# Delta-rule recurrence and gated experts on one core: gates' exponential and rank comparison ordered four slots later, softmax sums of two experts inverted together

## The chip, the cores and the metric

The kernel runs on 1 core of a Trainium2 chip. The metric is the device time of one execution in microseconds, the median of several runs. Engines are named as the profile names them: PE is TensorE, DVE VectorE, ACT ScalarE, POOL GpSimd, SP the engine that issues transfers.

## The reference

A recurrence over 768 steps, for 4 batches of 8 heads, gives `x` of 4 x 768 x 320. Then four small attention experts work on `x`; each row (token) uses the two experts with the largest gate:

```python
logits = x @ w_gate
topk = np.argpartition(-logits, K, axis=-1)[..., :K]     # K = 2 of E = 4
sel = sel - sel.max(-1, keepdims=True)
w = np.exp(sel)
w /= w.sum(-1, keepdims=True) + 1e-09
for e in range(E):
    scores = scale * (q @ k.transpose(0, 2, 1))          # causal
    a = np.exp(scores - scores.max(-1, keepdims=True))
    a /= a.sum(-1, keepdims=True) + 1e-09
    out += mask[..., None] * w[:, :, kk:kk + 1] * (a @ v @ wo[e])
```

## The kernel before

The first part, `recurrence`, computes `x` in chunks up to about 385 us of the profiled execution; its order is written out by hand and the change leaves it alone. The second part, `moe`, is the experts.

**Units.** The experts' work is 48 units, one for each batch b (4), block j of 256 rows (3) and expert e (4), in the order of `UNITS`; units 2p and 2p+1 are always the two experts of one pair, an even and an odd one, with the same rows. A unit has two row tiles t. For each, `scores` (L806) multiplies queries and keys into a PSUM tile `sc` (two buffers), VectorE adds the causal mask and takes the row's extreme (L813, which frees `sc`), and ScalarE takes the exponential with the row's sum (L815). `norm` then adds 1e-9 to the two sums (L820), inverts them (L821), GpSimd multiplies the inverse by the token's gate (L822) and the whole tile `P` by the result (L826, two multiplications of 128 to 768 columns). TensorE transposes `P` (L834) three units later, ScalarE (L840) or VectorE (L838) copies the transposes to SBUF, and four units later `mix` (L852) multiplies them with the values, for both experts of the pair at once. `fin` (L863) applies the output weights.

**Batch preparation.** While the units of one batch run, the pieces of the next batch's projections are filled in between (`FILL`): `l`/`s` load and split `x` (VectorE cast L706, then GpSimd L707 and L708), `k` the queries and keys (L729, copied out of PSUM by ScalarE L737 and VectorE L738), `v` the values and the gates' logits (L748, L751, L752). All of them and the transposes share three PSUM buffers named `pt`.

**The gates.** For a batch, `rank` compares the four logits of each token with one another on VectorE (L766) and counts on GpSimd how many are larger (L768, L770, nine small additions and subtractions after one another, "the counts" below); `shift` takes the maximum (L774), subtracts it on GpSimd (L775) and turns the counts into a 0/1 choice on VectorE (L776, "the comparison"); `gate` takes the exponential on ScalarE (L779), multiplies by the choice on GpSimd (L780), and VectorE sums and inverts (L781 to L783) before GpSimd scales (L784). Batch 0 does this in two halves, the others once each.

**The order.** Each piece of the program is a slot; `later(d, f)` places an operation d slots after the one that asks for it, with `DL, DE, DN, DR` as the distances. From this written order the compiler's scheduler makes one fixed queue for each engine, in which an operation may stand earlier or later than written; at run time every engine works through its queue in order and waits where an operand isn't ready.

```python
LAG = (3, 4, 6)
DL, DE, DN, DR = 1, 3, 4, 1
            later(DE, lambda: A.activation(P[:, 0:n], P[:, 0:n], AF.Exp, bias=m[:, 0, t:t + 1], scale=-1.0, accum_out=m[:, 1, t:t + 1]))
            if t == 1:
                later(DN, norm)
```

Of the kernel before, what the change touches and what calls it, by code (L numbers as in the profile page):

```python
# [7 lines left out]
F32 = mybir.dt.float32  # L8
AF = mybir.ActivationFunctionType
OP = mybir.AluOpType  # L10
# [580 lines left out]

DL, DE, DN, DR = 1, 3, 4, 1

# [64 lines left out]
def moe(tc, ctx, I, xT, out, ident, pre, FL=None, FI=None):  # L658
# [10 lines left out]
    def later(d, f):  # L669
        due.setdefault(now[0] + d, []).append(f)  # L670
# [45 lines left out]
    def proj(b):  # L716
# [37 lines left out]
        gs = {}  # L754
        def rank(a, i=slice(0, 6)):

            L = G[b][:, i]
            if a == 0:
                gs["R"] = sp.tile([128, 6, 4], F32, name="gr", bufs=2)
                gs["c"] = sp.tile([128, 3, 6, 3], F32, name="gc", bufs=1)  # L760
                gs["m"] = sp.tile([128, 2, 6], F32, name="gm", bufs=2)
                for d in range(4):
                    PL.memset(gs["R"][:, i, d], 3.0 - d)
            R, c = gs["R"][:, i], gs["c"][:, a, i]
            n = c.shape[1]
            V.tensor_tensor(c[:, :, 0:3 - a], L[:, :, a:a + 1].to_broadcast([128, n, 3 - a]), L[:, :, a + 1:4], op=OP.is_ge)  # L766
            def count():
                PL.tensor_tensor(R[:, :, a + 1:4], R[:, :, a + 1:4], c[:, :, 0:3 - a], op=OP.add)  # L768
                for d in range(3 - a):
                    PL.tensor_tensor(R[:, :, a], R[:, :, a], c[:, :, d], op=OP.subtract)  # L770
            later(DR, count)
        def shift(i=slice(0, 6)):
            L, R, mx = G[b][:, i], gs["R"][:, i], gs["m"][:, 0, i]
            V.tensor_reduce(mx, L, axis=AX.X, op=OP.max)  # L774
            PL.tensor_tensor(L, L, mx[:, :, None].to_broadcast(L.shape), op=OP.subtract)  # L775
            V.tensor_scalar(R, R, 1.5, None, op0=OP.is_lt)  # L776
        def gate(i=slice(0, 6)):
            L, R, mx, c = G[b][:, i], gs["R"][:, i], gs["m"][:, 0, i], gs["m"][:, 1, i]
            A.activation(L, L, AF.Exp)  # L779
            PL.tensor_tensor(L, L, R, op=OP.mult)  # L780
            V.tensor_reduce(mx, L, axis=AX.X, op=OP.add)  # L781
            V.tensor_scalar(mx, mx, 1e-9, None, op0=OP.add)
            V.reciprocal(c, mx)  # L783
            PL.tensor_tensor(L, L, c[:, :, None].to_broadcast(L.shape), op=OP.mult)  # L784
        half = lambda x: slice(3 * x, 3 * x + 3)
# [3 lines left out]

    OT, PT = {}, {}  # L790

    def unit(b, j, e, last):
# [3 lines left out]
        def scores(t):  # L796
# [10 lines left out]
            if t == 0:  # L807
                st["m"] = sp.tile([128, 4, 2], F32, name="m", bufs=10)
                st["P"] = [None, None]
            m = st["m"]  # L810
            P = st["P"][t] = sp.tile([128, 768], F32, name="P", bufs=8)
# [3 lines left out]
            later(DE, lambda: A.activation(P[:, 0:n], P[:, 0:n], AF.Exp, bias=m[:, 0, t:t + 1], scale=-1.0, accum_out=m[:, 1, t:t + 1]))  # L815
            if t == 1:
                later(DN, norm)
        def norm():
            m = st["m"]
            V.tensor_scalar(m[:, 2], m[:, 1], 1e-9, None, op0=OP.add)  # L820
            V.reciprocal(m[:, 2], m[:, 2])  # L821
            PL.tensor_tensor(m[:, 3], m[:, 2], G[b][:, 2 * j:2 * j + 2, e], op=OP.mult)  # L822
            for t in range(2):
                n = 128 * (2 * j + t + 1)
                P = st["P"][t]
                PL.tensor_tensor(P[:, 0:n], P[:, 0:n], m[:, 3, t:t + 1].to_broadcast([128, n]), op=OP.mult)  # L826
        def transp(z):
# [149 lines left out]
```

## Time and profile before

| what | value |
|---|---|
| time, median of 3 runs | 623.82 us (622.46 to 625.45) |
| the profiled execution's own time | 622.29 us |
| its span, first to last instruction | 620.5 us |
| mean granted TensorE clock | 0.942 of full speed |
| busy over the span: TensorE, VectorE, ScalarE, GpSimd | 88%, 75%, 77%, 59% |

All rows below come from that one profiled execution, whose own time is 1.53 us below the median. Times in rows are microseconds from the span's start. A timeline row gives the start, the duration (of merged rows, from the first start to the last end), engine, line, operation, tiles, count, and in brackets the engine's idle time before it and what ended that.

### The profile page before, as it was taken

The numbers are of one execution on the slowest core, as the hardware profiler recorded it, in microseconds if no ns is written. First come the engines' busy times: TensorE is split into PE (matmuls) and PEld (weight loads), VectorE is DVE, ScalarE is ACT, GpSimd is POOL, SyncE is SP. The second block draws the span as 40 slices with busy tenths as digits, with TensorE's granted clock in tenths as the row PEclk, the third lists the DMA queues.
The fourth block names the chain that finished last, engine by engine and source line by source line (L and its number), as shares of the span: only waits on it lengthen the run. The fifth ranks groups of instructions, "written<-read, shape, count | busy, mean of one in ns | idle before, by whom it ended". The sixth has DMA issues, their size and how long they took to land.

```text
span 620.5 us, 22307 instructions
## 1 busy us (share of the span) xinstructions
PE 545.8 (88%) x8753; PEld 477.8 (77%) x8753; DVE 468.5 (75%) x1137; ACT 478.9 (77%) x1299; POOL 366.0 (59%) x600
## 2 busy tenths in 40 slices
PE   5564799998898889889999999889999979999996
PEld 5454688887787778778888778768888868888884
DVE  7977768899999979997567773776785567567752
ACT  7992569899879878988999995677775577677763
POOL 2321299759968989998880020586854646463851
PEclk9555579999999999999999999999999989999999
DMA  7884344676578566646338943432131132202111
GB/s 198 226 191 109 99 108 117 140 202 157 121 178 208 141 143 186 155 102 183 88 94 242 235 115 111 109 90 64 50 109 38 50 80 58 69 1 52 43 37 57
DMA packets 63690, 73.77 MB, mean 119 GB/s; under 512 B 30168, under 2 KB 48344, under 8 KB 63576
## 3 DMA queue, kind: packets, MB, share of 16 engines
q1 hardware_dynamic: 63432, 72.15, 45.1%
q8 instruction: 72, 1.18, 0.8%
q14 instruction: 42, 0.34, 0.2%
q10 hardware_dynamic: 144, 0.10, 0.1%
HBM read 54.92 MB, written 11.01 MB: 106 GB/s over the span
## 4 chain that ended last, share of the span: by engine, by line
PE 51%; ACT 19%; POOL 10%; DVE 10%; issue 6%; DMA 4%; SPq 0%; POOLq 0%; DVEq 0%; ACTq 0%
PE py L415 6%; PE ot L852 6%; PE pt L729 6%; PE sc L806 4%; PE pt L834 4%; PE pt L863 4%; PE pt L748 3%; POOL MT L319 3%; POOL TP L319 3%; PE pt L441 3%; ACT GT L386 3%; PE ps L392 3%; ACT LS L445 3%; PE ps L405 3%; PE ps L383 3%
## 5 line engine op out<-in xcount | busy, mean ns | idle before, releaser
L319 POOL TENSOR_TENSOR MT<-MT,TP 128x30 f32<-128x30 f32 (+9 forms) x150 | 99.2, 662 | 11.8
L319 POOL TENSOR_TENSOR TP<-MT 128x30 f32<-128x30 f32 (+9 forms) x150 | 92.1, 614 | 11.6
L826 POOL TENSOR_TENSOR P<-P,m 128x128 f32<-128x128 f32 (+2 forms) x96 | 88.5, 943 | 3.5
L415 PE MATMUL py<-R,LS 128*40 128x80 f32 x1536 | 85.4, 238 | 3.4 <-issue 0.8
L813 DVE CUSTOM_DVE_ANT_0 P<-sc,MK 128x128 f32<-128x128 f32 (+2 forms) x96 | 59.5, 623 | 24.3 <-PE sc L806 14.5
L408 DVE TENSOR_TENSOR R<-ps,CM 64x128 f32<-64x128 f32 x192 | 54.9, 286 | 23.7 <-PE ps L405 20.1
L415 PEld LDWEIGHTS py<-R,LS 128*40 128x40 f32 x1536 | 63.8, 119 | 11.6 <-ACT LS L445 5.3
L815 ACT ACTIVATE P<-P,m 128x128 f32<-128x128 f32 (+2 forms) x96 | 63.8, 665 | 11.5 <-DVE m L813 10.7
L806 PE MATMUL sc<-ks,qs 128*128 128x384 f32 (+4 forms) x256 | 61.2, 343 | 1.9 <-DVE m L813 1.9
L394 ACT ACTIVATE R<-ps 32x160 f32<-32x160 f32 x192 | 56.6, 295 | 5.6 <-PE ps L392 1.5
L386 ACT ACTIVATE GT<-ps 32x160 f32<-32x160 f32 x192 | 56.4, 294 | 3.4
L834 PE MATMUL pt<-CM,P 128*128 128x128 f32 x336 | 52.6, 277 | 6.3 <-ACT pt L840 5.1
L822 POOL TENSOR_TENSOR m<-m,gg 128x2 f32<-128x2 f32 x48 | 10.8, 224 | 78.1 <-DVE m L821 54.8
L392 PE MATMUL ps<-GT,TT 128*33 128x80 f32 x768 | 47.0, 244 | 3.3 <-DVE TT L321 1.3
L376 ACT ACTIVATE LS<-pt 64x320 f32<-64x320 f32 x96 | 41.4, 432 | 9.8 <-PE pt L372 8.3
L834 PEld LDWEIGHTS pt<-CM,P 128*128 128x128 f32 x336 | 40.1, 141 | 11.4 <-ACT pt L840 6.2
L405 PE MATMUL ps<-RB,VU 128*64 128x64 f32 x768 | 46.1, 229 | 3.0 <-ACT VU L400 1.9
L445 ACT ACTIVATE LS<-pt 40x320 f32<-40x320 f32 x92 | 39.6, 430 | 10.8 <-PE pt L441 7.8
L806 PEld LDWEIGHTS sc<-ks,qs 128*128 128x128 f32 x256 | 40.8, 191 | 4.1 <-DVE m L813 3.1
L729 PE MATMUL pt<-xh,wq 128*128 128x384 f32 x192 | 41.5, 349 | 2.0 <-DVE xh L706 1.2
L405 PEld LDWEIGHTS ps<-RB,VU 128*64 128x64 f32 x768 | 36.1, 139 | 8.6 <-ACT VU L400 7.8
L283 PE MATMUL ps<-AB,KB 40*64 40x32 f32 x512 | 26.3, 274 | 18.5 <-DVE AB L258 12.8
(159 smaller groups left out, 1346.6 us busy)
## 6 DMA issues: line engine op xcount, KB each, us to landing
RB<-in_RB SPq DMA_DIRECT2D x24, 320.0 KB
EK<-in_EK SPq DMA_DIRECT2D x18, 416.0 KB
ks<-ks SPq DMA_DIRECT2D x32, 192.0 KB
R<-in_VG SPq DMA_DIRECT2D x24, 208.0 KB
EW<-in_EA SPq DMA_DIRECT2D x18, 214.5 KB
R<-in_VT SPq DMA_DIRECT2D x48, 80.0 KB
R<-in_RT SPq DMA_DIRECT2D x24, 160.0 KB
xT<-XT SPq DMA_DIRECT2D x48, 80.0 KB
```

The costliest lines, as they stand in the source:

```text
L319: return [lambda: e.tensor_tensor(tmp, row, col, op=OP.mult), lambda: e.tensor_tensor(o, o, tmp, op=OP.add)]
L386: A.activation(gt[b:b + 32, s::2], p_g[64 * s:64 * s + 32], AF.Copy)
L392: T.matmul(p_u[64 * x:64 * x + 33, y], tt[:, o:o + 33], gt[:, 2 * p:2 * p + 2], start=True, stop=True, tile_position=(0, 64 * x))
L405: T.matmul(p_f[64 * x:64 * x + 64, y], vu[:, p, :], rb[:, 4 * g + p, :], start=True, stop=True, tile_position=(0, 64 * x))
L415: T.matmul(py[64 * s:64 * s + 40, p], ls[:, h, :], m, start=True, stop=True, tile_position=(0, 64 * s))
L445: A.activation(o, x, AF.Copy)
L729: T.matmul(p, w, x, start=(j == 0), stop=(j == len(prs) - 1))
L806: T.matmul(ps[:, c, 0:cw], QS[b][:, e, o], KS[b][:, e, z, k], start=(z == 0), stop=(z == 1))
L813: V.tensor_tensor_reduce(pv, ps[:, 0:ch, 0:cw], MK[:, 768 - n:768].rearrange("p (c k) -> p c k", c=ch), 1.0, 3e38, OP.add, OP.min, m[:, 0, ...
L815: later(DE, lambda: A.activation(P[:, 0:n], P[:, 0:n], AF.Exp, bias=m[:, 0, t:t + 1], scale=-1.0, accum_out=m[:, 1, t:t + 1]))
L826: PL.tensor_tensor(P[:, 0:n], P[:, 0:n], m[:, 3, t:t + 1].to_broadcast([128, n]), op=OP.mult)
L834: T.transpose(p[:, 128 * y:128 * y + 128], st["P"][t][:, 128 * c:128 * c + 128], ident)
```

## The change

In the gates, the counts are no longer placed one slot after each comparison of logits but are written by `shift` itself, after the subtraction of the maximum; the exponential (L779 before, L776 after) and the comparison (L776 before, L777 after) are placed `DR` = 4 slots later, the multiplication by the choice 4 slots after `gate`'s own slot, and sum, inverse and scaling 8 slots after it. In the units, `norm` is no longer called for each unit but once for a pair, by the odd one: 1e-9, inverse and product with the gates act on four sums of the pair, and GpSimd then multiplies the even unit's two tiles and after them the odd unit's.

```diff
@@ -589,7 +589,7 @@
 
 LAG = (3, 4, 6)
 
-DL, DE, DN, DR = 1, 3, 4, 1
+DL, DE, DN, DR = 1, 3, 4, 4
 
 FIRST = "l1 k1 v0 k0 s1 v2 v1 R0 R1 R2 k2 H0 k3 G0"
 FILL0 = "k4 k7", "k6 v4 k5", "v3", "v5 R3 R4 R5 H1", "G1", "", "", "", "", "", "", ""
@@ -764,30 +764,34 @@
             R, c = gs["R"][:, i], gs["c"][:, a, i]
             n = c.shape[1]
             V.tensor_tensor(c[:, :, 0:3 - a], L[:, :, a:a + 1].to_broadcast([128, n, 3 - a]), L[:, :, a + 1:4], op=OP.is_ge)
-            def count():
-                PL.tensor_tensor(R[:, :, a + 1:4], R[:, :, a + 1:4], c[:, :, 0:3 - a], op=OP.add)
-                for d in range(3 - a):
-                    PL.tensor_tensor(R[:, :, a], R[:, :, a], c[:, :, d], op=OP.subtract)
-            later(DR, count)
         def shift(i=slice(0, 6)):
             L, R, mx = G[b][:, i], gs["R"][:, i], gs["m"][:, 0, i]
             V.tensor_reduce(mx, L, axis=AX.X, op=OP.max)
             PL.tensor_tensor(L, L, mx[:, :, None].to_broadcast(L.shape), op=OP.subtract)
-            V.tensor_scalar(R, R, 1.5, None, op0=OP.is_lt)
+            for a in range(3):
+                c = gs["c"][:, a, i]
+                PL.tensor_tensor(R[:, :, a + 1:4], R[:, :, a + 1:4], c[:, :, 0:3 - a], op=OP.add)
+                for d in range(3 - a):
+                    PL.tensor_tensor(R[:, :, a], R[:, :, a], c[:, :, d], op=OP.subtract)
+            later(DR, lambda: A.activation(L, L, AF.Exp))
+            later(DR, lambda: V.tensor_scalar(R, R, 1.5, None, op0=OP.is_lt))
         def gate(i=slice(0, 6)):
             L, R, mx, c = G[b][:, i], gs["R"][:, i], gs["m"][:, 0, i], gs["m"][:, 1, i]
-            A.activation(L, L, AF.Exp)
-            PL.tensor_tensor(L, L, R, op=OP.mult)
-            V.tensor_reduce(mx, L, axis=AX.X, op=OP.add)
-            V.tensor_scalar(mx, mx, 1e-9, None, op0=OP.add)
-            V.reciprocal(c, mx)
-            PL.tensor_tensor(L, L, c[:, :, None].to_broadcast(L.shape), op=OP.mult)
+            def pick():
+                PL.tensor_tensor(L, L, R, op=OP.mult)
+            def total():
+                V.tensor_reduce(mx, L, axis=AX.X, op=OP.add)
+                V.tensor_scalar(mx, mx, 1e-9, None, op0=OP.add)
+                V.reciprocal(c, mx)
+                PL.tensor_tensor(L, L, c[:, :, None].to_broadcast(L.shape), op=OP.mult)
+            later(DR, pick)
+            later(2 * DR, total)
         half = lambda x: slice(3 * x, 3 * x + 3)
         return dict(l=lambda n: load(b, n), s=lambda n: split(b, n), k=lambda i: qk((0, 2, 1, 3)[i % 4], i // 4)(), v=lambda i: vg(i)(),
                     r=rank, h=lambda i: shift(), g=lambda i: gate(), R=lambda x: rank(x % 3, half(x // 3)),
                     H=lambda x: shift(half(x)), G=lambda x: gate(half(x)))
 
-    OT, PT = {}, {}
+    OT, PT, PAIR = {}, {}, {}
 
     def unit(b, j, e, last):
 
@@ -805,25 +809,28 @@
                 for z in range(2):
                     T.matmul(ps[:, c, 0:cw], QS[b][:, e, o], KS[b][:, e, z, k], start=(z == 0), stop=(z == 1))
             if t == 0:
-                st["m"] = sp.tile([128, 4, 2], F32, name="m", bufs=10)
+                if s == 0:
+                    PAIR[b, j, ep] = (sp.tile([128, 4, 2, 2], F32, name="m", bufs=4), [])
                 st["P"] = [None, None]
-            m = st["m"]
+                PAIR[b, j, ep][1].append(st["P"])
+            m = PAIR[b, j, ep][0][:, :, s]
             P = st["P"][t] = sp.tile([128, 768], F32, name="P", bufs=8)
             pv = P[:, 0:n].rearrange("p (c k) -> p c k", c=ch)
             V.tensor_tensor_reduce(pv, ps[:, 0:ch, 0:cw], MK[:, 768 - n:768].rearrange("p (c k) -> p c k", c=ch), 1.0, 3e38,
                                    OP.add, OP.min, m[:, 0, t:t + 1])
             later(DE, lambda: A.activation(P[:, 0:n], P[:, 0:n], AF.Exp, bias=m[:, 0, t:t + 1], scale=-1.0, accum_out=m[:, 1, t:t + 1]))
-            if t == 1:
+            if t == 1 and s == 1:
                 later(DN, norm)
         def norm():
-            m = st["m"]
+            m, Ps = PAIR[b, j, ep]
             V.tensor_scalar(m[:, 2], m[:, 1], 1e-9, None, op0=OP.add)
             V.reciprocal(m[:, 2], m[:, 2])
-            PL.tensor_tensor(m[:, 3], m[:, 2], G[b][:, 2 * j:2 * j + 2, e], op=OP.mult)
-            for t in range(2):
-                n = 128 * (2 * j + t + 1)
-                P = st["P"][t]
-                PL.tensor_tensor(P[:, 0:n], P[:, 0:n], m[:, 3, t:t + 1].to_broadcast([128, n]), op=OP.mult)
+            PL.tensor_tensor(m[:, 3], m[:, 2], G[b][:, 2 * j:2 * j + 2, 2 * ep:2 * ep + 2].rearrange("p t e -> p e t"), op=OP.mult)
+            for x in range(2):
+                for t in range(2):
+                    n = 128 * (2 * j + t + 1)
+                    P = Ps[x][t]
+                    PL.tensor_tensor(P[:, 0:n], P[:, 0:n], m[:, 3, x, t:t + 1].to_broadcast([128, n]), op=OP.mult)
         def transp(z):
 
             if z == 0:
```

What this does to the engines' queues is shown at three places (lines of the changed kernel: L766, L769, L777, L783 to L785 are the gates on VectorE, L770, L773, L775 on GpSimd; L819 is the mask, L828 and L833 the products with the gate and with `P`).

GpSimd where the gates of the third batch are made (about 485 to 497 us of the trace), before:

```order
L826 TENSOR_TENSOR P<-P,m 128x640
L826 TENSOR_TENSOR P<-P,m 128x768
L822 TENSOR_TENSOR m<-m,gg 128x2
L826 TENSOR_TENSOR P<-P,m 128x640
L826 TENSOR_TENSOR P<-P,m 128x768
L707 TENSOR_TENSOR xh<-x,xh 64x384
L708 TENSOR_TENSOR x<-x,xh 128x768
L768 TENSOR_TENSOR gr<-gr,gc 128x6x3
```

and after the change:

```order
L707 TENSOR_TENSOR xh<-x,xh 64x384
L828 TENSOR_TENSOR m<-m,gg 128x4
L708 TENSOR_TENSOR x<-x,xh 128x768
L833 TENSOR_TENSOR P<-P,m 128x640
L833 TENSOR_TENSOR P<-P,m 128x768
L833 TENSOR_TENSOR P<-P,m 128x640
L833 TENSOR_TENSOR P<-P,m 128x768
L770 TENSOR_TENSOR gg<-gg,gm 128x24
L773 TENSOR_TENSOR gr<-gr,gc 128x6x3
```

The split of `x` (L707, L708) now stands ahead of the products with `P` of the even unit; those of both units stand ahead of the counts, which begin with the last row.

VectorE at the same place, before:

```order
L813 ISA P,m<-sc,MK 128x512
L813 ISA m 128x1
L776 TENSOR_SCALAR gr<-gr 128x24
L781 TENSOR_REDUCE gm<-gg 128x6
L782 TENSOR_SCALAR gm<-gm 128x6
L783 RECIPROCAL gm<-gm 128x6
L820 TENSOR_SCALAR m<-m 128x2
L813 ISA P,m<-sc,MK 128x384
L813 ISA m 128x1
L821 RECIPROCAL m<-m 128x2
L738 SCALAR_TENSOR_TENSOR qs<-pt,qs 64x384 x2
```

and after the change:

```order
L819 ISA P,m<-sc,MK 128x512
L819 ISA m 128x1
L777 TENSOR_SCALAR gr<-gr 128x24
L819 ISA P,m<-sc,MK 128x384
L819 ISA m 128x1
L738 SCALAR_TENSOR_TENSOR qs<-pt,qs 64x384 x2
L819 ISA P,m<-sc,MK 128x512
L819 ISA m 128x1
```

The comparison (L777) still stands ahead of the next mask of 384 columns and of the two operations on `qs` that empty a `pt` buffer; the gates' sum and inverse have left this place.

VectorE where the gates of the second batch are made (about 430 to 436 us), before:

```order
L774 TENSOR_REDUCE gm<-gg 128x6
L813 ISA P,m<-sc,MK 128x640
L813 ISA m 128x1
L738 SCALAR_TENSOR_TENSOR qs<-pt,qs 64x384 x2
L813 ISA P,m<-sc,MK 128x768
L813 ISA m 128x1
L838 COPY pt<-pt 128x384
L776 TENSOR_SCALAR gr<-gr 128x24
L706 CAST xh<-x 128x1152
```

and after the change:

```order
L769 TENSOR_REDUCE gm<-gg 128x6
L777 TENSOR_SCALAR gr<-gr 128x24
L783 TENSOR_REDUCE gm<-gg 128x6
L784 TENSOR_SCALAR gm<-gm 128x6
L785 RECIPROCAL gm<-gm 128x6
L819 ISA P,m<-sc,MK 128x640
L819 ISA m 128x1
L738 SCALAR_TENSOR_TENSOR qs<-pt,qs 64x384 x2
L819 ISA P,m<-sc,MK 128x768
L819 ISA m 128x1
L845 COPY pt<-pt 128x384
L706 CAST xh<-x 128x1152
```

The comparison, which stood behind two masks and a copy, now stands ahead of all of them, with the gates' sum and inverse right behind it; the cast (L706) keeps its place behind the copy.

## Rows read from the trace of the kernel before

**Rows 1.** Engines' busy time over the experts' stretch, 381 to 621 us (us, instructions).

```profile
381.00:621.00 240.00, 221.11 (x1585) 192.33 (x1585) 155.71 (x467) 158.57 (x422) 130.47 (x230) 0.99 0.23 64
```

**Rows 2.** TensorE's waits in that stretch: us in total, times, longest.

```profile
PE pt L834 <- ACT pt L840: 5.1, 3, 3.7
```

**Rows 3.** Groups by shape, 381 to 621 us: busy us, mean ns, idle before.

```profile
L820 DVE TENSOR_SCALAR m<-m 128x2 f32<-128x2 f32 x48 | 15.3, 319 | 15.8 <-ACT P L815 15.2
...
L822 POOL TENSOR_TENSOR m<-m,gg 128x2 f32<-128x2 f32 x48 | 10.8, 224 | 78.1 <-DVE m L821 54.8 <-PE sc L806 11.7 <-DVE m L820 4.5
```

**Rows 4.** Timeline of GpSimd, 486 to 516 us: start, us, operation, idle before.

```profile
489.63 2.68 POOL L826 TENSOR_TENSOR P<-P,m 128x640 f32<-128x640 f32 x2
492.39 1.01 POOL L707 TENSOR_TENSOR xh<-x,xh 64x384 fp32r<-64x384 f32 x1
...
495.26 0.22 POOL L768 TENSOR_TENSOR gr<-gr,gc 128x18 f32<-128x18 f32 x1
```

**Rows 5.** Timeline of VectorE, same stretch.

```profile
488.74 0.76 DVE L706 CAST xh<-x 128x1152 fp32r<-128x1152 f32 x1
...
496.82 0.18 DVE L776 TENSOR_SCALAR gr<-gr 128x24 f32<-128x24 f32 x1 [3.63 <-POOL gr L770]
...
498.84 1.12 DVE L738 SCALAR_TENSOR_TENSOR qs<-pt,qs 64x384 fp32r<-64x384 f32 x2
```

**Rows 6.** Timeline of ScalarE, same stretch.

```profile
497.00 0.22 ACT L779 ACTIVATE gg<-gg 128x24 f32<-128x24 f32 x1 [4.36 <-POOL gg L775]
```

**Rows 7.** Timeline of TensorE, same stretch.

```profile
499.48 0.55 PE L834 MATMUL pt<-CM,P 128*128 128x128 f32 x3 [3.66 <-ACT pt L840]
500.01 1.96 PE L729 MATMUL pt<-xh,wq 128*128 128x384 f32 x6
```

**Rows 8.** Busy time by stretch; the bare number before DMA's share is TensorE's granted clock.

```profile
500.00:503.00 3.00, 3.00 (x13) 2.98 (x13) 1.94 (x7) 1.83 (x6) 1.85 (x3) 0.57 0.00 0
```

**Rows 9.** Timelines of GpSimd, VectorE and TensorE, 546 to 566 us.

```profile
549.28 2.68 POOL L826 TENSOR_TENSOR P<-P,m 128x640 f32<-128x640 f32 x2
552.15 0.22 POOL L768 TENSOR_TENSOR gr<-gr,gc 128x18 f32<-128x18 f32 x1 [0.19 <-DVE gc L766]
...
553.71 0.18 DVE L776 TENSOR_SCALAR gr<-gr 128x24 f32<-128x24 f32 x1 [0.79 <-POOL gr L770]
...
555.73 1.12 DVE L738 SCALAR_TENSOR_TENSOR qs<-pt,qs 64x384 fp32r<-64x384 f32 x2
...
556.91 1.31 PE L729 MATMUL pt<-xh,wq 128*128 128x384 f32 x6
```

**Rows 10.** Timelines of VectorE, ScalarE, GpSimd and TensorE, 426 to 442 us.

```profile
429.94 0.34 DVE L766 TENSOR_TENSOR gc<-gg 128x18 f32<-128x18 f32 x3
...
435.62 0.75 DVE L706 CAST xh<-x 128x1152 fp32r<-128x1152 f32 x1
...
433.58 0.22 ACT L779 ACTIVATE gg<-gg 128x24 f32<-128x24 f32 x1 [1.74 <-POOL gg L775]
...
436.81 1.01 POOL L707 TENSOR_TENSOR xh<-x,xh 64x384 fp32r<-64x384 f32 x1
...
439.84 2.69 POOL L826 TENSOR_TENSOR P<-P,m 128x640 f32<-128x640 f32 x2
...
434.48 0.55 PE L834 MATMUL pt<-CM,P 128*128 128x128 f32 x3 [1.05 <-ACT pt L840]
...
441.65 0.60 PE L834 MATMUL pt<-CM,P 128*128 128x128 f32 x4
```

**Rows 11.** Timelines of VectorE, GpSimd and TensorE at the end, 580 to 621 us.

```profile
606.84 0.62 DVE L820 TENSOR_SCALAR m<-m 128x2 f32<-128x2 f32 x1 [0.27 <-ACT P L815]
...
606.47 0.97 POOL L826 TENSOR_TENSOR P<-P,m 128x128 f32<-128x128 f32 x2
...
606.43 1.50 PE L834 MATMUL pt<-CM,P 128*128 128x128 f32 x10
608.04 1.74 PE L852 MATMUL ot<-pt,vv 128*64 128x256 f32 x16
```

## Prediction, made before the changed kernel ran

> **What bounds the kernel now.** I read the busy times first, then TensorE's waits, then the timelines of all engines around each wait. In the experts' stretch TensorE is busy for 221.1 of 240 us, the other engines for 130 to 159 [rows 1]; some 6 us of what is missing lie behind its last matmul. So a change to VectorE, ScalarE or GpSimd is worth only what it adds to or takes from TensorE's few waits. The largest class of these is 5.1 us in three pieces, TensorE waiting for ScalarE to empty a PSUM buffer `pt` [rows 2]; 3.66 us of it is one wait at 499.48 [rows 7], behind which the granted clock is 0.57 for 3 us [rows 8]. Its cause stands in ScalarE's timeline: it sat idle for 4.36 us before the gates' exponential, until GpSimd had subtracted the maximum [rows 6]. GpSimd was late because the counts stood behind two products with `P` and the split of `x` [rows 4]. VectorE waited 3.63 us for the same counts, at the comparison [rows 5]. The change aims at this, so the question is whether counts, comparison and what stands behind them come earlier.
>
> **Removed work.** 24 of the 48 additions of 1e-9, as many inverses and as many small products go. The additions cost VectorE 319 ns each and the small products GpSimd 224 ns [rows 3]: 7.7 and 5.4 us for 24. They hide under TensorE, which waits for neither on the average: VectorE sat idle 15.8 us before these additions, GpSimd 78.1 us before the products [rows 3]. I count zero; were each a piece of a wait of TensorE's, it could be a gain of 1 us at most, since TensorE's waits outside the places below are short.
>
> **Moved work, the price.** The even unit's two products with `P` no longer run while the odd unit is computed. They start after the odd unit's inverse, and the odd unit's come behind them, so GpSimd has four products in a row: 2.68 us for each unit of 640 and 768 columns [rows 4, 9], 5.36 for a pair. Where the counts follow, they come later by a unit's products. I time GpSimd from start to start: from the first count (495.26) to the comparison that waits for the last (496.82) it is 1.56 us [rows 4, 5], and the same 1.56 from 552.15 to 553.71 [rows 9]. With the subtraction moved among them I take 1.73.
>
> *Gates of the third batch (about 490 us).* On GpSimd the split of `x` now stands ahead of both units' products. It needs the cast, which ends at 489.5 [rows 5] and a little sooner when the inverse stands behind it: 489.4. The two instructions of the split take 2.87 us (492.39 to 495.26) [rows 4], with the small product some 3.0. Products run from 492.4 to 497.8, the counts until 499.55. The comparison is 2.7 us later than its 496.82 [rows 5]. ScalarE is free, since its exponential now stands behind a copy, and the wait of 3.66 us as such is gone. But the next projection (L729) needs a `pt` buffer that VectorE empties (L738), and that stands behind the comparison: now it runs 498.84 to 499.96 and L729 starts at 500.01 [rows 5, 7]. After the change one mask stands between (the five small operations have left, so less than today's 2.02 us; I take 0.7): L738 from 500.25 to 501.35, L729 at 501.4. **Plus 1.4 us**; with 2.02 kept it would be 2.7, and if the cast and split come 1.4 earlier, nothing.
>
> *Gates of the fourth batch (about 550 us).* Order on VectorE and ScalarE stays nearly as it was. The products run from 549.28 to 554.64 instead of to 551.96, the counts end at 556.4, and the comparison waits until then instead of 553.71 [rows 9]. From comparison to L738 it is 2.02 us, L738 takes 1.12, and L729 starts right behind it at 556.91 [rows 9]. So L729 starts at 559.4 to 559.5. **Plus 2.4 us**; bounds 1.5 and 2.7, because a wait of 0.6 us behind it may shrink.
>
> *Gates of the second batch (about 435 us).* Here the counts stand ahead of the products and start when the logits are compared (429.94) [rows 10]; they end at 431.85, so ScalarE's wait for them and TensorE's 1.05 us behind it go [rows 10]. But the comparison and the gates' sum now hold up both masks, the copy and the cast: comparison 431.85, two us to L738 as in [rows 9], 1.12 for it, mask and copy behind, cast at about 436.5 instead of 435.62. The split (436.81) has 0.44 us to spare behind the cast and slips by 0.5. Behind it the even unit's products now stand where the odd unit's were (439.84 to 442.53) [rows 10], so they end at about 443.05. Its transposes start at 441.65 [rows 10]; they had their products long before and now wait for them. **Plus 1.4 us**, the recovered 1.05 counted in; bounds 0.5 and 2.0.
>
> *End.* The last pair's sums are ready at 606.84 [rows 11]; the even unit's products, now 606.47 to 607.44, start behind the inverse at about 607.55 (GpSimd no longer works beside it, so the addition takes less than its 0.62) and end at 608.5. Three of the ten transposes from 606.43 need them, and the next mix, at 608.04 [rows 11], follows: 608.95. Nothing is left behind it to absorb this. **Plus 0.9 us**, bounds 0.4 and 1.4.
>
> **Sum.** 1.4 + 2.4 + 1.4 + 0.9 = 6.1 us; by the lower bounds 2.4, by the upper 8.8. On the profiled execution's own 622.29 us this gives 628.4. That execution lies 1.5 us below the median, so against the median I forecast **629.9 us**.
>
> **The clock.** The sum leaves the half-speed spell at 500 us in place: TensorE now would wait from about 497.8 to 501.4, as long as the 3.66 us that stood ahead of 0.57 of the clock [rows 7, 8]. There six matmuls L729 took 1.96 us, and 1.31 at the full 2.4 GHz [rows 7, 9]; with 1.2 GHz as the lower level, 3 us at 0.57 lose some 1.3. The wait of 1.05 us at 434.48 is shorter than the two new ones, 2.4 us at 441 and nearly 3 at 556, so no row says what those do. The Trainium skill, "TensorE: Matmul & The Clock Gate", section "HAM oscillation — how this bites in real kernels", says that TensorE falls back to the half clock when it is left waiting, and that this is paid again for each such wait. [...]
>
> **Rivals.**
> 1. *Falls of the clock at the two new waits.* Two falls at the 1.3 to 1.7 us that the one at 500 costs add about 3: 633. For it: the row at 500; against it: both waits are shorter. Chance 0.15.
> 2. *ScalarE was the real holder, so the kernel gets faster.* Place: the waits of 3.66 at 499.48 and 1.05 at 434.48. It decides if the counts of the third batch end by 496.8 as they do now, so that L738 isn't held; then 3.66 + 1.05 + 1.3 of clock = 6.0 are gained: 617.8. For it: the idle 4.36 us [rows 6]. Against it: the comparison still stands ahead of L738, behind four products. Chance 0.14.
> 3. *The terms come out small.* If VectorE, relieved of 24 additions, runs the cast and the masks a microsecond earlier at each place, and the wait at 490 us is split in two so that the clock doesn't fall there, about 2.5 is left: 626.3, which counts as no change. Chance 0.16.
> 4. *The move does nothing*: the scheduler kept the comparison at its old place at two of three gates, so this part of the change does not do what its distance says. It is in the forecast.
>
> **How the numbers follow.** The forecast has 0.55: with rival 1 slower has 0.70. About 0.5% (3.1 us) is what a measurement of this kernel can tell from no change; 623.8 less or more that is 620.7 and 626.9. Faster is rival 2, 0.14; same is rival 3, 0.16. The forecast's own range is 626.5 to 633. The range of 8 in 10 takes in rivals 1 and 3 and leaves out rival 2 and a little above rival 1: 621 to 635.
>
> **What would show it.** Right: in the changed profile the comparison at the third and fourth batch's gates waits for GpSimd until 2 to 3 us later within its place, TensorE's largest waits are for VectorE's L738 at L729 and for products with `P` at the transposes near 441 and at the end; ScalarE's idle time before the gates' exponential is small. Wrong: if TensorE's wait at 490 to 502 us is under 2 us in sum, rival 2 or 3 holds; if the granted clock falls near 443 or 559, rival 1.

## The result, and the profile after

The changed kernel takes 631.6 us (median of four runs, 629.1 to 635.26) against 623.14 us for the kernel before: a ratio of 1.0132, 95% interval 1.0091 to 1.0173. It is slower by some 8 us. The forecast was 629.9 us and slower, so sign and size came out; of the steps behind them some held and three did not. One of the four runs of `after_gates_on_vectore` below, 623.66 us, counts as slow, over 1.5% above the fastest, and is left out of its median.

The profiled execution took 629.1 us, its span is 627.3 us, and before they were 622.29 and 620.5. The recurrence, which the change leaves alone, took 3.9 us less in this execution; over all profiled executions of this document it takes 388.6 to 395.5 us, so this is the spread between executions. So I compare the **experts' stretch**: from the first `scores` matmul to the end. The first fence is the busy time by stretch of the kernel before, the second of the changed kernel; columns are the stretch, its length, then busy time and count of TensorE, its weight loads, VectorE, ScalarE, GpSimd, and the granted clock of TensorE.

```profile
392.51:620.50 227.99, 210.90 (x1512) 182.70 (x1511) 149.53 (x447) 152.62 (x406) 127.84 (x215) 0.99 0.21 58
```

```profile
388.60:627.31 238.71, 218.20 (x1512) 187.15 (x1511) 139.46 (x399) 153.06 (x406) 120.75 (x191) 0.96 0.20 56
407.70:411.10 3.40, 3.40 (x14) 2.51 (x12) 2.09 (x11) 2.82 (x8) 1.82 (x4) 0.52 0.00 0
441.80:445.20 3.40, 3.40 (x18) 2.21 (x18) 1.92 (x5) 2.37 (x5) 1.95 (x3) 0.53 0.33 81
496.40:499.80 3.40, 3.19 (x13) 2.37 (x15) 0.00 (x0) 1.75 (x5) 3.40 (x7) 0.53 0.00 0
503.30:506.70 3.40, 3.40 (x16) 3.40 (x15) 2.46 (x12) 2.66 (x7) 1.85 (x3) 0.52 0.00 0
561.30:564.70 3.40, 2.93 (x11) 2.79 (x10) 2.49 (x7) 1.62 (x6) 0.68 (x2) 0.52 0.02 5
```

The stretch is 10.72 us longer. The same 1512 matmuls were busy 7.30 us longer, and TensorE's idle time rose by only 3.42 us (17.09 to 20.51, length less busy time). The longer matmuls are the clock: five stretches at about half of 2.4 GHz, where before there was one [rows 8]. But the 7.30 us are not the price of the falls: a matmul that runs slowly where TensorE would have waited anyway only fills the wait (the last section has such a place). What each place cost is read from starts, in the table below. VectorE, meanwhile, is busy 10 us less, and no gain from it can be seen.

TensorE's waits in the changed kernel, 381 to 628 us (us in total, times, longest):

```profile
PE pt L841 <- POOL P L833: 5.1, 7, 1.2
PE sc L810 <- DVE m L819: 2.8, 2, 2.5
PE pt L729 <- DVE qs L738: 2.3, 2, 1.8
PE pt L841 <- ACT pt L847: 2.1, 1, 2.1
```

Against [rows 2], the 5.1 us for ScalarE became 2.1, the transposes' waits for products with `P` are now the largest class, and the projection L729 waits for VectorE's copy of `qs` (L738). Four places follow, as timelines of all engines. *Third batch's gates:*

```profile
492.65 2.51 DVE L766 TENSOR_TENSOR gc<-gg 128x18 f32<-128x18 f32 x3
493.86 5.34 POOL L833 TENSOR_TENSOR P<-P,m 128x640 f32<-128x640 f32 x4
495.19 0.33 PE L841 MATMUL pt<-CM,P 128*128 128x128 f32 x1 [0.61 <-POOL P L833]
496.61 0.90 PE L841 MATMUL pt<-CM,P 128*128 128x128 f32 x3 [1.09 <-POOL P L833]
500.90 0.18 DVE L777 TENSOR_SCALAR gr<-gr 128x24 f32<-128x24 f32 x1 [5.05 <-POOL gr L775]
501.57 1.12 DVE L738 SCALAR_TENSOR_TENSOR qs<-pt,qs 64x384 fp32r<-64x384 f32 x2
502.25 0.21 ACT L776 ACTIVATE gg<-gg 128x24 f32<-128x24 f32 x1
502.75 1.76 PE L729 MATMUL pt<-xh,wq 128*128 128x384 f32 x6 [1.84 <-DVE qs L738]
```

This is the chain that was forecast: four products in a row, then the counts, then the comparison after 5.05 us of waiting (3.63 before, [rows 5]), one mask, L738, and L729 right behind it. ScalarE's exponential waits for nobody any more (4.36 us before, [rows 6]), and it doesn't help. *Fourth batch's gates:*

```profile
552.04 5.33 POOL L833 TENSOR_TENSOR P<-P,m 128x640 f32<-128x640 f32 x4
558.43 0.22 ACT L776 ACTIVATE gg<-gg 128x24 f32<-128x24 f32 x1 [2.91 <-POOL gg L770]
559.07 0.18 DVE L777 TENSOR_SCALAR gr<-gr 128x24 f32<-128x24 f32 x1 [2.34 <-POOL gr L775]
560.90 0.55 PE L841 MATMUL pt<-CM,P 128*128 128x128 f32 x3 [2.15 <-ACT pt L847]
561.92 2.29 PE L729 MATMUL pt<-xh,wq 128*128 128x384 f32 x6 [0.47 <-DVE qs L738]
```

Here GpSimd's lateness reaches TensorE in two ways: ScalarE's exponential waits 2.91 us for the subtraction, and of TensorE's waits the 2.15 us are for ScalarE; VectorE's comparison waits 2.34 us, and the 0.47 us are for L738, which ends last. The six matmuls L729 take 2.29 us here and took 1.31 in [rows 9]: that is the half clock. *Second batch's gates:*

```profile
429.93 0.18 DVE L777 TENSOR_SCALAR gr<-gr 128x24 f32<-128x24 f32 x1 [1.58 <-POOL gr L775]
438.40 5.33 POOL L833 TENSOR_TENSOR P<-P,m 128x640 f32<-128x640 f32 x4
439.73 0.33 PE L841 MATMUL pt<-CM,P 128*128 128x128 f32 x1 [1.20 <-POOL P L833]
441.15 0.55 PE L841 MATMUL pt<-CM,P 128*128 128x128 f32 x3 [1.10 <-POOL P L833]
```

The two products of the even unit end 1.4 us apart, and TensorE waits for one after the other. *First batch, second half of the gates*, a place that the prediction did not price:

```profile
402.99 1.90 POOL L833 TENSOR_TENSOR P<-P,m 128x128 f32<-128x128 f32 x4
406.50 0.17 DVE L777 TENSOR_SCALAR gr<-gr 128x12 f32<-128x12 f32 x1 [2.45 <-POOL gr L775]
407.33 0.79 PE L810 MATMUL sc<-ks,qs 128*128 128x512 f32 x2 [2.53 <-DVE m L819]
```

Here VectorE's late comparison holds up a mask, the mask keeps the buffer `sc`, and TensorE waits 2.53 us. Before, it waited 1.65 us there:

```profile
411.19 0.74 PE L806 MATMUL sc<-ks,qs 128*128 128x512 f32 x2 [1.65 <-DVE m L813]
```

Two waits for products stood ahead of that one then, 0.63 and 0.24 us, so that the sum is the same, 2.52 us. What is new is the fall behind it. *The end:*

```profile
612.98 0.17 DVE L826 TENSOR_SCALAR m<-m 128x4 f32<-128x4 f32 x1 [0.41 <-ACT P L821]
614.18 0.33 PE L841 MATMUL pt<-CM,P 128*128 128x128 f32 x1 [0.62 <-POOL P L833]
614.75 0.44 PE L841 MATMUL pt<-CM,P 128*128 128x128 f32 x2 [0.24 <-POOL P L833]
615.12 1.74 PE L859 MATMUL ot<-pt,vv 128*64 128x256 f32 x16
```

By place, with the shift of the same matmuls' starts from the one profile to the other:

| place | forecast | TensorE's waits before | after | shift measured |
|---|---|---|---|---|
| first batch, ~407 | 0 | 0.63, 0.24, 1.65 | 2.53 | +1.9, one fall of the clock in it |
| second batch, ~440 | +1.4 | 1.05 | 1.20, 1.10 | +3.0, one fall in it |
| third batch, ~500 | +1.4 | 3.66, one fall behind it | 0.61, 1.09, 1.84 | +1.85, two falls in it |
| fourth batch, ~560 | +2.4 | 0.42, 0.60 | 2.15, 0.47 | +2.3 to L729's start, +2.95 behind the fall, where the wait of 0.60 is gone |
| ~590 | 0 | none | 0.21 | +0.4 |
| end | +0.9 | as [rows 11] | 0.62, 0.24 | +0.93 |

### The profile page after: what moved, and what is told of

Read it like the earlier page. It is cut to its first block, busy times and chain, and to the rows that moved or that the text cites. A ratio compares the mean times of both kernels' runs of the same rounds, so it can differ in the third digit from the quotient of the medians.

```text
span 627.3 us, 22220 instructions
## 1 busy us (share of the span) xinstructions
PE 550.6 (88%) x8753; PEld 480.0 (77%) x8753; DVE 456.7 (73%) x1089; ACT 480.0 (77%) x1299; POOL 360.4 (57%) x576
## 4 chain that ended last, share of the span: by engine, by line
PE 41%; ACT 10%; DVE 6%; POOL 5%; issue 4%; DMA 2%; POOLq 0%; SPq 0%; ACTq 0%; DVEq 0%
PE ot L859 6%; PE pt L729 6%; PE sc L810 4%; PE py L415 4%; PE pt L841 4%; PE pt L870 4%; PE pt L748 3%; POOL P L833 2%; PE pt L441 2%; PE ps L383 2%; PE ps L405 2%; ACT LS L445 2%; PE ps L392 2%; ACT GT L386 2%; ACT R L394 1%
## 5 line engine op out<-in xcount | busy, mean ns | idle before, releaser
L319 POOL TENSOR_TENSOR TP<-MT 128x30 f32<-128x30 f32 (+9 forms) x150 | 93.4, 623 | 11.6
L833 POOL TENSOR_TENSOR P<-P,m 128x128 f32<-128x128 f32 (+2 forms) x96 | 86.7, 935 | 1.6
L819 DVE CUSTOM_DVE_ANT_0 P<-sc,MK 128x128 f32<-128x128 f32 (+2 forms) x96 | 58.8, 622 | 31.6 <-PE sc L810 20.1
L841 PE MATMUL pt<-CM,P 128*128 128x128 f32 x336 | 54.8, 283 | 7.4 <-POOL P L833 5.1
L841 PEld LDWEIGHTS pt<-CM,P 128*128 128x128 f32 x336 | 41.1, 144 | 13.3 <-POOL P L833 7.1
L828 POOL TENSOR_TENSOR m<-m,gg 128x4 f32<-128x4 f32 x24 | 5.3, 219 | 72.9 <-DVE m L827 64.1
L729 PE MATMUL pt<-xh,wq 128*128 128x384 f32 x192 | 42.9, 358 | 3.9 <-DVE qs L738 2.3
L859 PE MATMUL ot<-pt,vv 128*64 128x256 f32 (+1 forms) x384 | 44.3, 370 | 0.0
L847 ACT ACTIVATE pt<-pt 128x512 f32<-128x512 f32 (+1 forms) x64 | 34.5, 541 | 11.7 <-PE pt L841 10.7
```

Source lines behind the costliest of these rows:

```text
L319: return [lambda: e.tensor_tensor(tmp, row, col, op=OP.mult), lambda: e.tensor_tensor(o, o, tmp, op=OP.add)]
L729: T.matmul(p, w, x, start=(j == 0), stop=(j == len(prs) - 1))
L819: V.tensor_tensor_reduce(pv, ps[:, 0:ch, 0:cw], MK[:, 768 - n:768].rearrange("p (c k) -> p c k", c=ch), 1.0, 3e38, OP.add, OP.min, m[:, 0, ...
L833: PL.tensor_tensor(P[:, 0:n], P[:, 0:n], m[:, 3, x, t:t + 1].to_broadcast([128, n]), op=OP.mult)
L841: T.transpose(p[:, 128 * y:128 * y + 128], st["P"][t][:, 128 * c:128 * c + 128], ident)
L859: T.matmul(po[h, 128:256] if one else po[h], VV[b][:, k, 2 * ep + s], P[:, 256 * k:256 * k + (128 if one else 256)], start=(k == 0), stop= ...
```

## Experiments

Theory P: the pairs cost, by four products in a row on GpSimd ahead of the counts. Theory G: the gates' reordering costs. Every kernel ran beside the kernel before on one chip. The last two columns are of the profiled execution's experts' stretch, read as in the first two fences.

| kernel | median us | ratio to before, 95% | stretch us | TensorE busy us |
|---|---|---|---|---|
| before | 623.1 to 624.6 | | 227.99 | 210.90 |
| changed | 631.6 | 1.0132 [1.0091, 1.0173] | 238.71 | 218.20 |
| gates_only | 623.31 | 0.9987 [0.9954, 1.002] | 229.37 | 212.35 |
| pairs_only | 631.6 | 1.0109 [1.005, 1.0167] | 237.70 | 217.02 |
| after_comparison_on_gpsimd | 628.45 | 1.0058 [1.0032, 1.0084] | 234.38 | 215.21 |
| after_inverse_per_unit | 636.1 | 1.0176 [1.0128, 1.0225] | 240.08 | 215.98 |
| after_last_pair_per_unit | 635.51, one run | | 238.18 | 217.02 |
| before_gates_on_vectore | 615.18 | 0.9862 [0.9804, 0.992] | 222.22 | 209.67 |
| the same again | 616.34 | 0.9874 [0.9835, 0.9913] | | |
| after_gates_on_vectore | 616.66 | 0.9852 [0.9774, 0.9929] | 223.30 | 210.11 |
| before_counts_on_vectore | 615.44 | 0.9878 [0.9837, 0.992] | 222.38 | 208.72 |
| after_counts_on_vectore | 619.29 | 0.9925 [0.9902, 0.9949] | 224.59 | 210.37 |

**One half of the change at a time.** `gates_only` is the kernel before with the diff's first two pieces (`DR` and the gates), `pairs_only` with the others (`PAIR`, `norm`). In `gates_only` the first products of batch 0 take gates that are not yet scaled, because without the pairs they are written ahead of the scaling; instructions and sizes are the same.

> Only the gates' part of the change: counts written behind the subtraction, exponential and comparison placed four slots later, sum and inverse eight; the softmax sums are inverted for each unit as before. Theory P (the pairs cost: four products with P in a row on GpSimd hold the counts, these hold VectorE's comparison and the copy of qs behind it, and TensorE's clock falls behind each new wait): the queues of TensorE and ScalarE stay as they were apart from one exponential, VectorE's comparison keeps its neighbours at the three later gates, so 622 to 625 us, one half-speed spell in the experts' stretch, near 500 us, and TensorE's wait of 3.7 us there. Theory G (the gates' move costs): 628 to 632 us, with the waits for the copy of qs at 3 us near 500 and 560.

> Only the pairs' part: one addition, one inverse, one small product for two units, then four products with P; the gates as before. Theory P: 629 to 634 us, with TensorE waiting for products with P near 440 and 497, for the copy of qs near 503 and 562, and a half-speed spell behind each. Theory G: 622 to 626 us.

Measured: 623.31 us, no difference to before, and 631.6 us, the changed kernel's time, with the four spells that were expected. Theory G is out. The queues say why the gates' half is worth nothing: in `gates_only` VectorE's comparison stands between the same neighbours as before at all three later gates, GpSimd's subtraction has only moved in among the counts, and ScalarE's gates' exponential stands where it stood. The scheduler took "four slots later" back. In `gates_only` TensorE still waits for ScalarE at the third batch, 2.92 us where 3.7 were expected. Not expected was a second spell, behind the wait of 1.64 us at the first batch's gates, where the kernel before waits 1.65 us and keeps its clock:

```profile
499.45 0.55 PE L838 MATMUL pt<-CM,P 128*128 128x128 f32 x3 [2.92 <-ACT pt L844]
```

```profile
410.80 0.73 PE L810 MATMUL sc<-ks,qs 128*128 128x512 f32 x2 [1.64 <-DVE m L817]
```

```profile
412.30:415.70 3.40, 3.40 (x15) 2.81 (x14) 2.28 (x7) 2.13 (x5) 2.82 (x8) 0.52 0.16 34
```

**The gates off GpSimd.** Ranks by one comparison of all four logits with all four, summed along the row, and subtraction, choice and scaling on VectorE, in the kernel before and in the changed one (with it `gr` has one buffer instead of two, and in the kernel before `m` has eight instead of ten):

```diff
+                V.tensor_tensor(c, L[:, :, None, :].to_broadcast([128, n, 4, 4]), L[:, :, :, None].to_broadcast([128, n, 4, 4]), op=OP.is_gt)
+                V.tensor_reduce(gs["R"][:, i], c, axis=AX.X, op=OP.add)
-            PL.tensor_tensor(L, L, mx[:, :, None].to_broadcast(L.shape), op=OP.subtract)
+            V.tensor_tensor(L, L, mx[:, :, None].to_broadcast(L.shape), op=OP.subtract)
...
```

> The kernel before, but nothing of the gates runs on GpSimd: one comparison of all four logits with all four and a sum along the row give the counts on VectorE, and the subtraction, the choice and the scaling are VectorE's too. Theory P: counts behind products are what holds TensorE at 499 us already before the change, so its wait of 3.66 us, the half-speed spell behind it (1.3 to 1.7 us) and perhaps the 1.05 us at 434 go: 616 to 620 us. Theory G, and any by which VectorE is the scarce engine: the added VectorE work (some ten small operations for each batch) gives back what is won: 622 to 626 us.

> The changed kernel, but nothing of the gates runs on GpSimd, as in the run before_gates_on_vectore. Theory P: the terms at the third and fourth batch's gates (1.4 and 2.4 us with the spells behind them) go and with them the wait of before at 499 us; left are the transposes that wait for products near 440, the place near 407 and the 0.9 us at the end: 621 to 625 us, some 3 to 5 us above before_gates_on_vectore. If the late products themselves hold the transposes everywhere, and not the gates behind them: 627 to 631 us.

Measured: 615.18 and 616.66 us, both below the ranges of theory P (616 to 620 and 621 to 625): it had the sign right and too small a gain. Both are faster than both kernels of the change. Which of the two is faster the times don't tell: the intervals overlap. The 3 to 5 us that theory P expected between them are missing: in the stretch the pairs cost 9.7 us with the gates on GpSimd (`pairs_only`) and 1.1 us here. The busy time by stretch, of the kernel before with this edit and then of the changed one:

```profile
390.91:613.13 222.22, 209.67 (x1512) 180.87 (x1511) 154.69 (x457) 153.62 (x408) 118.60 (x158) 1.00 0.22 60
```

```profile
392.65:615.95 223.30, 210.11 (x1512) 181.12 (x1511) 139.18 (x408) 153.98 (x408) 111.29 (x134) 0.99 0.22 60
```

No half-speed spell is left in either stretch until the last microseconds. VectorE is busy 15.5 us less in the second, and the stretch is no shorter: relieving VectorE shows no yield here, though a small gain could hide behind the price of the late products. What the pairs add by themselves are products that the transposes wait for:

```profile
439.89 0.55 PE L835 MATMUL pt<-CM,P 128*128 128x128 f32 x3 [1.10 <-POOL P L827]
492.24 0.33 PE L835 MATMUL pt<-CM,P 128*128 128x128 f32 x1 [0.51 <-POOL P L827]
493.69 0.55 PE L835 MATMUL pt<-CM,P 128*128 128x128 f32 x3 [1.12 <-POOL P L827]
```

The kernel before with this edit was measured again, in more rounds:

> The same kernel as before_gates_on_vectore, measured again in five rounds: 614 to 617 us, a ratio of 0.983 to 0.990 to the kernel before.

Measured: 616.34 us, ratio 0.9874; it stands.

**Is VectorE's comparison the link?** One instruction of the changed kernel on another engine:

```diff
-            later(DR, lambda: V.tensor_scalar(R, R, 1.5, None, op0=OP.is_lt))
+            later(DR, lambda: PL.tensor_scalar(R, R, 1.5, None, op0=OP.is_lt))
```

> The changed kernel with one instruction moved to another engine: the comparison of the counts with 1.5 runs on GpSimd, behind the counts, instead of on VectorE. At the third batch's gates nothing that waits for GpSimd is then left on VectorE ahead of the copy of qs; at the fourth the gates' sum still stands ahead of it, behind one more GpSimd operation. If it is VectorE's wait for the counts that TensorE feels (theory P): TensorE's wait of 1.84 us for the copy of qs near 503 goes with one half-speed spell there (some 3 us together), the waits for products with P near 440 and 497 stay, the wait near 561 stays or grows by 0.2 to 0.6: 626 to 630 us. If TensorE is held by ScalarE or by the products alone, the wait near 503 stays under another name: 630 to 634 us.

Measured: 628.45 us, as theory P has it, and its interval lies below that of the changed kernel. TensorE at the third batch:

```profile
500.19 0.55 PE L841 MATMUL pt<-CM,P 128*128 128x128 f32 x3 [1.09 <-POOL P L833]
...
502.68 1.30 PE L729 MATMUL pt<-xh,wq 128*128 128x384 f32 x6
```

From that transpose to L729 it is 2.49 us instead of 6.14 (496.61 to 502.75 in the changed kernel), with no wait and no fall. The wait of 2.53 us for `sc` near 407 went as well, though the expectation didn't name it: it hung on the same comparison, in the first batch. So the gain is that of two places, less a fall at 397 us that the changed kernel's profile doesn't have (behind waits of 1.62 and 1.27 us for the split and the gates' sum of batch 0). At the fourth batch, where the gates' sum still stands ahead of L738 and ScalarE's exponential still waits for GpSimd, TensorE's waits are 2.15 and 0.55 us, much as in the changed kernel.

**The inverse for each unit, the products in pairs:**

```diff
-            if t == 1 and s == 1:
-                later(DN, norm)
+            if t == 1:
+                later(DN, invert)
+            if t == 1 and s == 1:
+                later(DN, norm)
```

> The changed kernel with the addition of 1e-9 and the inverse done for each unit as before (48 of each on VectorE); small product and the four products with P stay in pairs. It gives back all that the sharing saves on VectorE and keeps the late products; the scheduler puts the split of the third batch behind the four products instead of ahead of them. If the sharing is worth nothing and the late products cost (theory P): 630 to 635 us, no less than the changed kernel. If the additions were a gain that hides part of the cost: 634 to 640 us. If the long wait for the pair's inverse is the cost, 624 to 627 us.

Measured: 636.1 us, 1.1 us above theory P's range and in that of the second case, that the additions had been a gain. But it isn't a clean test: the scheduler put the split behind the four products at the third batch, so the counts ended later still, and the wait there became the longest of all kernels:

```profile
494.05 5.90 POOL L837 TENSOR_TENSOR P<-P,m 128x640 f32<-128x640 f32 x4
500.03 1.00 POOL L707 TENSOR_TENSOR xh<-x,xh 64x384 fp32r<-64x384 f32 x1
```

```profile
505.60 0.55 PE L845 MATMUL pt<-CM,P 128*128 128x128 f32 x3 [4.33 <-ACT pt L851]
```

Its interval also overlaps that of the changed kernel. So it doesn't tell what the sharing is worth; the two kernels with the gates on VectorE, above, come nearest to that.

**The end alone**: `norm` for each unit in the last pair of the program.

> The changed kernel, the last pair of the program alone normed for each unit as before; on all other places the queues are those of the changed kernel. The term of 0.9 us at the end is tried by itself: TensorE's two waits for products with P in the last pair (0.62 and 0.24 us) go, and the time from the last pair's first transpose to the end falls by 0.8 to 0.9 us. If the end is set by the output's way out and not by TensorE, it stays as it is.

Measured: the wait of 0.62 us went, that of 0.24 stayed, and from the last `mix` ahead of these transposes to the last output matmuls it took 6.79 us instead of 7.28, so 0.5 of the 0.93 us came back. The pair ahead still brings four products in a row, and they run beside the even unit's addition, which took 0.84 us for 0.17:

```profile
618.30 0.84 DVE L828 TENSOR_SCALAR m<-m 128x2 f32<-128x2 f32 x1 [0.45 <-ACT P L821]
```

**Length of the counts, or place behind the products?** The comparison of four with four and its sum on VectorE, but subtraction, choice and scaling on GpSimd as they were:

> The kernel before, counts by one comparison of all four logits with all four and a sum on VectorE; the subtraction of the maximum, the choice and the scaling stay on GpSimd, behind its products and the split. It parts the length of the counts (1.56 us on GpSimd) from the place of the gates behind other work. If the length is what held (theory L): almost all of the gain of before_gates_on_vectore comes, 615 to 618 us. If the place is (theory P): ScalarE's exponential still waits for a subtraction that stands behind two products and the split, only some 1.5 us less, so a wait of 1.5 to 2.5 us near 499 is left, with or without a half-speed spell: 619 to 623 us.

> The changed kernel with the same edit. Theory L: as after_gates_on_vectore, 616 to 620 us. Theory P: at the third batch nothing on VectorE ahead of the copy of qs waits for GpSimd, so TensorE's wait near 503 goes; at the fourth batch the gates' sum stands ahead of that copy and waits for subtraction, exponential and choice behind four products, so that TensorE still waits 1 to 2.5 us near 560, perhaps with a half-speed spell: 621 to 626 us.

TensorE's waits for ScalarE, of the kernel before with this edit (third batch) and of the changed one (fourth batch):

```profile
492.92 0.55 PE L828 MATMUL pt<-CM,P 128*128 128x128 f32 x3 [2.24 <-ACT pt L834]
```

```profile
552.05 0.55 PE L835 MATMUL pt<-CM,P 128*128 128x128 f32 x3 [1.44 <-ACT pt L841]
```

Measured: 615.44 us, as theory L says, and 619.29 us, inside theory L's range and below theory P's. For the kernel before, theory P had the mechanism and missed the price: the wait that it names is there (2.24 us, on ScalarE), but no half-speed spell follows, and 1.65 us at 411, which it left out, went too (waits of before: 3.66, 1.65, 1.05; after this edit: 2.24, none, 0.70). In the changed kernel the wait that is left at the fourth batch is 1.44 us, at the low end of theory P's 1 to 2.5. Taking the 1.56 us of counts off GpSimd brings, in the kernel before, all that taking the whole gates off it brings, and in the changed one most of it. But the edit does two things at once: it shortens GpSimd's work, and VectorE's comparison no longer waits for GpSimd at all. In the changed kernel the second alone (`after_comparison_on_gpsimd`) takes the ratio from 1.0132 to 1.0058, both together to 0.9925. For the kernel before the two were not parted.

## Why the prediction was right, and where it was wrong

**Right: which part of the work costs, and by which chain.** Four products in a row, counts behind them, comparison behind the counts, L738 behind the comparison, L729 behind L738: that is the profile of the third batch, and `after_comparison_on_gpsimd` shows that cutting the chain at the comparison frees it. Three terms came out close: the fourth batch 2.4 against 2.3 to L729's start (its own rows give 2.5 to 2.6, 559.4 to 559.5 less 556.91), the end 0.9 against 0.93, the second batch 1.4 against 1.4 with the fall apart (3.0 less 1.62, below). At the fourth batch the larger wait was for ScalarE, not for L738 as the prediction's sign has it. The third batch's 1.4 was 1.85: mask and copy came as reckoned (0.67 us from comparison to L738, 0.7 taken), but the comparison was 3.2 us later in its place (500.90 against 496.82 [rows 5], less 0.89 by which TensorE was late already), not 2.7. TensorE's one long wait there became three, 3.54 us in sum.

**Wrong: that the waits bring no new falls of the clock.** The prediction left the one spell at 500 us in place and put none into its sum for the two new waits, because no row of before had waits of 2 to 3 us to judge by; falls there are its first rival, at a chance of 0.15. By its own sign (the clock falls near 443 or 559) that rival is what the changed profile shows: spells from 441.8 and from 561.3, and two more. From the shifts, some 4 of the 11 us are falls: 1.57 in the first batch, 1.62 in the second, 0.7 in the fourth (2.95 less 2.26), nothing in the third. The price taken for one, 1.3 to 1.7 us, holds, and two pairs of runs show it. At the first batch's gates, behind the same wait, the changed kernel fell and `pairs_only` did not. Of `pairs_only`:

```profile
412.20:415.60 3.40, 3.36 (x19) 2.71 (x20) 2.63 (x11) 3.24 (x9) 1.22 (x3) 1.00 0.02 5
```

```profile
412.24 0.73 PE L806 MATMUL sc<-ks,qs 128*128 128x512 f32 x2 [2.54 <-DVE m L815]
...
416.59 0.49 PE L837 MATMUL pt<-CM,P 128*128 128x128 f32 x3
```

From these `scores` to this transpose it is 4.35 us at the full clock, and 5.92 us in the changed kernel (407.33 to 413.25), so one fall costs 1.57 us. At the second batch `after_inverse_per_unit` has the same two waits, 1.20 and 1.10 us, and keeps its clock:

```profile
447.00:450.40 3.40, 3.40 (x31) 2.60 (x29) 2.12 (x6) 2.66 (x6) 2.37 (x2) 1.00 0.50 116
```

From the transpose behind the second wait to the next three L841 or L845 it takes 3.27 us (446.79 to 450.06), in the changed kernel 4.89 (441.15 to 446.04): 1.62 us for this fall. At the fourth batch all five profiles with pairs and with counts on GpSimd have a spell (granted clock 0.52 to 0.56).

**Left out: the first batch's gates.** They have the same chain at smaller tiles, and it stands in the trace of before as a wait of 1.65 us for the mask, behind a comparison that waited 2.58 us for GpSimd. I had looked at the three later gates alone. The shift there was 1.9 us, but 1.57 of it is the fall: in `pairs_only`, without one, the same matmuls shift by 0.35 us. And that fall can't be laid to the pairs with certainty, since `gates_only` has one at the same place, behind the wait of before.

**Why the total was near all the same.** In the profiled executions the shifts sum to 11 us, not 6.1. The four places that were priced make 6.4 of it without their falls (1.4 + 1.85 + 2.26 + 0.93), so the waits came out nearly to size; falls make some 4, the two places left out 0.8. The medians differ by 8.5; the profiles show that executions differ in where the clock falls and in the length of the recurrence, but how many falls the other runs of the changed kernel have isn't known. The forecast was set 1.5 us above that one execution, and the changed kernel's median 2.5 us above its own. That 629.9 lies so near 631.6 is in part luck: the waits were reckoned about right, the falls were left out, and 631.6 lies between the forecast and the 633 of its first rival.

**Wrong in its attribution: what the gates' half does.** The prediction credits the change with putting ScalarE's exponential behind a copy. The pairs do that, by way of the scheduler: the gates' half alone leaves that queue as it was. The fourth rival, that the comparison's new distance does nothing, was the fact at all three later gates.

**Rival 2 (ScalarE was the real holder) is out.** Its wait went and L729 came no earlier. `before_gates_on_vectore` shows what that rival had right: about the 6.0 us that it reckoned lay in these waits and the fall behind them (5.8 us of the stretch, 8 to 9 by the medians). They belonged to the gates on GpSimd, which held ScalarE and VectorE alike. **The removed work** was larger than the 7.7 us reckoned for the additions: they went from 15.3 us [rows 3] to 4.9 us. At a price of zero for all of it the priced places come out at 6.4 us for 6.1; no run parts it from the late products. Their group in the changed kernel, 381 to 628 us:

```profile
L826 DVE TENSOR_SCALAR m<-m 128x4 f32<-128x4 f32 x24 | 4.9, 203 | 9.9 <-ACT P L821 9.5
```

## What to carry to other kernels

When an operation waits on an engine that is off the critical path, ask what stands behind the waiting operation in its queue: here one comparison of 0.18 us carried GpSimd's lateness to VectorE's copies and from there to TensorE. Moving such a chain's start "some slots later" may change nothing where a scheduler orders the queues; taking the chain off the late engine (here a comparison of all with all and a sum, in place of nine small operations) won 1.2% over the kernel before. Before work is batched to save instructions, check that the engine which is relieved is waited for at all, and that the first half of the batch is not what others wait for.

## What the runs showed of the hardware that I had not expected

**The same wait may or may not be followed by a fall of the clock.** In the changed kernel a wait of 2.53 us was followed by 0.52, in `pairs_only` one of 2.54 us at the same place by 1.00; waits of 1.20 and 1.10 us by 0.53 in the changed kernel and by 1.00 in `after_inverse_per_unit`; one of 1.65 us by 1.00 before the change, and one of 1.64 us by 0.52 in `gates_only`. The Trainium skill, "TensorE: Matmul & The Clock Gate", section "HAM oscillation — how this bites in real kernels", tells of a kernel in which every wait for its transfers was followed by a fall. The two longest waits of this case, 3.66 us before the change and 4.33 us in `after_inverse_per_unit`, were each followed by a fall and agree; behind the shorter ones a fall is possible, not certain. **A fall ahead of a wait can cost nothing.** In the changed kernel TensorE ran at 0.53 from 496.4 to 499.8, and from the transpose at 496.61 to L729 took 6.14 us. In `after_last_pair_per_unit`, whose queues are the same there, the granted clock is 1.00 at that place, TensorE waits 2.52 instead of 1.84 us for L738, and the two starts (503.34 and 509.48) are again 6.14 us apart:

```profile
502.50:505.90 3.40, 2.38 (x17) 1.59 (x17) 1.51 (x4) 1.82 (x5) 3.40 (x4) 1.00 0.00 0
```

```profile
509.48 1.96 PE L729 MATMUL pt<-xh,wq 128*128 128x384 f32 x6 [2.52 <-DVE qs L738]
```

The end of GpSimd's chain sets L729 there, at either clock.

**Small VectorE operations can stretch to the end of a GpSimd operation beside them.** Three comparisons of logits (L766) take 0.34 us at 429.94 [rows 10] and 2.51 us at the third batch after the change: there the first ended at 493.93, when GpSimd's L708 ended (493.90), and the third at 495.16, when the first product with `P` ended (495.13). The addition of 1e-9 shows the same over the stretch: before, 31 of the 48 had no GpSimd operation beside them and took 0.16 us in the mean, 17 had one and took 0.60; after, 21 of the 24 had none and took 0.17, with twice the elements. That is why the mean fell from 319 ns [rows 3] to 203. The Trainium skill, "SBUF — State Buffer", section "Who interferes with whom", says that a VectorE operation with two SBUF inputs, or one in a two-port mode, shares a port pair with GpSimd, and that the later one blocks until the other has finished. The comparisons, which have two inputs in SBUF, agree; whether the addition ran in such a mode no row shows.
